# Splitting the solve's state in PSUM with TensorE and ScalarE, and reordering a unit's first steps, in a delta-rule attention and rational MoE kernel

## The chip, the cores and the metric

The kernel runs on one core of one Trainium2 chip. The metric is the device time of one execution in microseconds (us). Engines are named as the profile names them: PE is TensorE, DVE is VectorE, ACT is ScalarE, POOL is GpSimd, SP is the engine that issues most of the DMAs.

## The reference

Two layers follow each other. The first is a delta rule over 768 time steps, for 4 batches and 8 heads of width 48; its output, laid out as 3072 tokens of 384 numbers, goes through a two-layer network whose activation is a rational function.

```python
k_n = k / (np.linalg.norm(k, axis=-1, keepdims=True) + 1e-06)
for t in range(S):
    y[:, :, t] = np.einsum('bhd,bhde->bhe', q[:, :, t], state)
    v_old = np.einsum('bhde,bhd->bhe', state, kt)
    state = state + bt[:, :, :, None] * np.einsum('bhd,bhe->bhde', kt, vt - v_old)
...
h = x @ w_in
P = a[0] + a[1] * h + a[2] * h2 + a[3] * h3
Q = 1.0 + np.abs(b[0]) * np.abs(h) + np.abs(b[1]) * h2
g = P / (Q + 1e-06)
return (g @ w_out).astype(np.float32)
```

## The kernel before

**Numbers.** Almost every matmul is made of f16 operands that stand for f32 numbers: a value x is split into a first half hi = f16(x) and a second half lo = f16(x - hi), and a product is three matmul passes, hi*hi, lo*hi and hi*lo (`PASSES`). `split16` (line 223) writes the two halves: hi by ACT (line 228 or, with a scale, 230), lo by DVE or POOL (line 232 or, with a scale, 234). `mm3` (line 395) issues the three passes head by head, 48 matmuls for 16 (pair, head) slots; a pair is one half of the 4 batches, and each pair has its own PSUM bank.

**Chunks.** Time is cut into 12 chunks of 64 steps. In a chunk the delta rule becomes a triangular system, whose right side is the residual `rr` (from the values, less what the state gives for them). The diagonal 16x16 blocks of the system are inverted on DVE (`inverse`), and the solve goes through its four block rows. `solve_start` puts the product of `wbd` and `rr` into the PSUM tile `pu`. Then `solve_step` runs three times: it splits `pu`, scaled by the 0/1 column `zmask` that keeps one block row, into z (hi and lo), and adds the product of `ebd` and z to `pu` with 48 matmuls. `solved` splits the finished `pu` without a scale. `state_next` updates the state S from z (`pd`), and `outputs` makes y (`py`).

**From attention to tokens.** `tokens` finds the largest number in y (`xs`), makes from it the scale of the chunk, and transposes and splits y into `xT`. `scalars` then computes, in a row of some twenty operations on single columns that go back and forth between ACT (line 764) and DVE, the table `msc` (line 790) of per-column factors that every unit of this chunk needs.

**Units.** The network is cut into 96 units, 8 in each chunk, one for each 256 of the 2048 hidden columns. `hidden` is 18 matmuls into the PSUM tile `ph` (line 806). `numerator` makes from `ph` the start of numerator and denominator: u (lines 823, 826, 830) and w (825, 828, 829). `quotient` takes 1/Q as exp(-ln) on ACT (841, 842) and the two halves of g on DVE and POOL (845 to 853). `accumulate` is 12 matmuls into `po` (line 868).

**The order.** The code issues a unit's steps and pieces of the attention of later chunks in turns (`attention`, called once in each unit; `back` for the solve of the next chunk, with raised priority). The program's final order on each engine isn't the code's: a scheduler with a timeline of its own picks, engine by engine, the ready instruction of the highest priority, so a change in the kind or the order of a few instructions can move others. Each engine then works through its own list strictly in order. `ph` has two buffers, u, w and r have three each.

## Time and profile before

| | |
|---|---|
| median of 3 runs | 858.86 us (855.03 to 863.0) |
| the profiled execution | 857.44 us, with a span of 855.5 us |
| busy in the span | DVE 770.2, PE 624.5, ACT 593.4, POOL 467.6 us |
| mean granted clock of TensorE | 0.883 |

The span runs from the first to the last instruction; the profiled execution took 1.9 us more than it. From 0 to about 150 us the weights are loaded and split and chunk 0 is solved; the units run from about 150 us to the end. In a group's row stand the busy time in total, the mean of one instruction in ns, and after the bar the idle time of the engine just before these instructions with what ended it. Durations of neighbouring instructions overlap a little, so the mean of one times the count can exceed the busy time.

### The profile page before, as it was taken

The numbers are of one execution on the slowest core, as the hardware profiler recorded it, in microseconds if no ns is written. First come the engines' busy times: TensorE is split into PE (matmuls) and PEld (weight loads), VectorE is DVE, ScalarE is ACT, GpSimd is POOL, SyncE is SP. The second block draws the span as 40 slices with busy tenths as digits, with TensorE's granted clock in tenths as the row PEclk, the third lists the DMA queues.
The fourth block names the chain that finished last, engine by engine and source line by source line (L and its number), as shares of the span: only waits on it lengthen the run. The fifth ranks groups of instructions, "written<-read, shape, count | busy, mean of one in ns | idle before, by whom it ended". The sixth has DMA issues, their size and how long they took to land. (4 is left out here: it accounts for less than half of the span.)

```text
span 855.5 us, 23235 instructions
## 1 busy us (share of the span) xinstructions
PE 624.5 (73%) x9264; PEld 491.8 (57%) x9264; DVE 770.2 (90%) x1369; ACT 593.4 (69%) x1242; POOL 467.6 (55%) x430
## 2 busy tenths in 40 slices
PE   0230425865887697598878979888789889999885
PEld 0220424644666376476667757666677667776563
DVE  5999898899889969889899999998999998998896
ACT  4766666865666584685867777767768767887774
POOL 7665655454436345654764855746738455353622
PEclk9755555987899799889989999999989999999998
DMA  8997979966996976878879779579588572300000
GB/s 236 245 202 155 221 148 173 143 137 131 162 158 112 182 142 112 143 148 154 145 139 162 118 147 165 102 148 162 97 169 143 114 114 49 71 2 20 1 19 19
DMA packets 466508, 111.47 MB, mean 130 GB/s; under 512 B 431328, under 2 KB 463072, under 8 KB 466400
## 3 DMA queue, kind: packets, MB, share of 16 engines
q1 hardware_dynamic: 464224, 108.83, 68.5%
q8 instruction: 72, 1.18, 0.6%
q10 hardware_dynamic: 2176, 1.17, 0.4%
q14 instruction: 36, 0.29, 0.1%
HBM read 40.47 MB, written 26.23 MB: 78 GB/s over the span
## 5 line engine op out<-in xcount | busy, mean ns | idle before, releaser
L806 PE MATMUL ph<-xT,w_in 128*128 128x256 f16 x1728 | 225.6, 285 | 39.2 <-DVE mu L830 32.8
L868 PE MATMUL po<-w_out,mg 128*128 128x384 f16 x1152 | 219.0, 337 | 35.0 <-POOL mg L853 31.4
L806 PEld LDWEIGHTS <-w_in 128*128 128x128 f16 x1728 | 173.1, 102 | 76.7 <-DVE mu L830 34.9
L853 POOL TENSOR_TENSOR mg<-mu,mr 128x512 f16<-128x512 f32 x96 | 133.5, 1391 | 132.7 <-DVE mu L852 83.2
L868 PEld LDWEIGHTS <-mg 128*128 128x128 f16 x1152 | 109.3, 100 | 109.7 <-POOL mg L853 41.0
L823 ACT ACTIVATE mu<-ph,coef,msc 128x512 f32<-128x512 f32 x96 | 74.0, 771 | 49.4 <-POOL mg L853 20.2
L829 ACT ACTIVATE mw<-mw 128x512 f32<-128x512 f32 x96 | 60.4, 629 | 55.3 <-DVE mw L828 55.0
L848 DVE SCALAR_TENSOR_TENSOR mw<-mw,msc,mg 128x512 f32<-128x512 f32 x96 | 87.0, 907 | 0.7
L826 DVE TENSOR_TENSOR mu<-ph,mu 128x512 f32<-128x512 f32 x96 | 65.4, 681 | 19.4 <-ACT mr L825 14.0
L850 POOL TENSOR_TENSOR mu<-mu,mw 128x512 f32<-128x512 f32 x36 | 50.3, 1398 | 53.1 <-DVE mw L848 31.2
L403 PEld LDWEIGHTS <-kbd 128*128 128x128 f16 x1680 | 59.8, 102 | 25.5 <-issue 19.1
L828 DVE SCALAR_TENSOR_TENSOR mw<-mr,msc,ph 128x512 f32<-128x512 f32 x96 | 70.5, 735 | 0.0
L830 DVE SCALAR_TENSOR_TENSOR mu<-mu,msc,ph 128x512 f32<-128x512 f32 x96 | 70.4, 734 | 0.0
L841 ACT ACTIVATE mr<-mw,msc 128x512 f32<-128x512 f32 x96 | 69.0, 719 | 1.2
L403 PE MATMUL pu<-z,ebd 128*128 128x48 f16 x1728 | 53.7, 186 | 20.3 <-DVE z L234 14.9
L403 PEld LDWEIGHTS <-ebd 128*128 128x128 f16 x1728 | 52.8, 98 | 22.8 <-issue 21.5
L825 ACT ACTIVATE mr<-ph,msc 128x512 f32<-128x512 f32 x96 | 65.2, 679 | 0.0
L847 DVE SCALAR_TENSOR_TENSOR mg<-mu,msc,mr 128x512 f16<-128x512 f32 x60 | 59.3, 988 | 2.5 <-ACT mr L842 2.5
L842 ACT ACTIVATE mr<-mr 128x512 f32<-128x512 f32 x96 | 60.0, 625 | 1.1
L852 DVE SCALAR_TENSOR_TENSOR mu<-mu,msc,mw 128x512 f32<-128x512 f32 x60 | 55.7, 928 | 0.4
L403 PEld LDWEIGHTS <-wbd 128*128 128x128 f16 x1152 | 38.6, 101 | 28.3 <-issue 27.1
L232 POOL TENSOR_TENSOR mm<-m,mm 128x1024 f16<-128x1024 f32 x12 | 31.7, 2639 | 34.2 <-ACT mm L228 34.2
(198 smaller groups left out, 1313.7 us busy)
## 6 DMA issues: line engine op xcount, KB each, us to landing
wsi<-in_moe_w_in_dram SPq DMA_DIRECT2D x24, 256.0 KB, 5.2
xdk<-kn SPq DMA_DIRECT2D x24, 256.0 KB, 3.6
kbd<-tk SPq DMA_DIRECT2D x24, 256.0 KB, 4.5
gd<-g SPq DMA_DIRECT2D x24, 256.0 KB, 3.8
wso<-in_moe_w_out_dram SPq DMA_DIRECT2D x32, 192.0 KB, 3.8
xdq<-kn SPq DMA_DIRECT2D x24, 256.0 KB, 3.4
mbd<-mm SPq DMA_DIRECT2D x24, 256.0 KB, 5.8
wc<-img SPq DMA_DIRECT2D x24, 256.0 KB, 5.3
```

What stands on the lines that cost most here:

```text
L403: nc.tensor.matmul(dst[p][:, h], head(bd, lp, p * H + h), head(rt, rp, p * H + h), start=start and n == 0 and h == 0, stop=stop and n == l ...
L806: nc.tensor.matmul(ph[:, i], w_in[:, f2, wp, cc, i * P : (i + 1) * P], x[:, xp, cc], start=k == 0, stop=k == 3 * NCC - 1,)
L823: nc.scalar.activation(u, ph, AF.Identity, scale=A3, bias=a2)
L825: nc.scalar.activation(z, ph, AF.Abs, scale=B1)
L826: nc.vector.tensor_mul(u, ph, u)
L828: nc.vector.scalar_tensor_tensor(out=w, in0=z, scalar=B0, in1=ph, op0=ALU.add, op1=ALU.mult)
L829: nc.scalar.activation(w, w, AF.Abs)
L830: nc.vector.scalar_tensor_tensor(out=u, in0=u, scalar=A1, in1=ph, op0=ALU.add, op1=ALU.mult)
L841: nc.scalar.activation(r, w, AF.Ln, bias=Q0)
L848: nc.vector.scalar_tensor_tensor(out=w, in0=w, scalar=Q0, in1=g[:, 0], op0=ALU.add, op1=ALU.mult)
L853: nc.gpsimd.tensor_mul(g[:, 1], u, r)
L868: nc.tensor.matmul(po[p], g[:, gp, i, p * P : (p + 1) * P], w_out[:, f2, wp, i], start=f2 == lo and i == 0 and k == 0, stop=f2 == hi - 1 a ...
```

## The change

Three things are changed.

- The split of `pu` in the solve (three times in `solve_step`, once in `solved`). Before, ACT wrote hi and DVE computed lo from `pu` and hi. Now ACT writes hi, PE adds -hi to `pu` in place (one 128x384 matmul for each pair, with minus the identity as weights), ACT writes lo as a plain scaled copy of what is left in `pu`, the 48 matmuls of `mm3` follow, and in `solve_step` PE adds hi back to `pu` (two more matmuls, with the identity).
- The start of a unit. Before, ACT made u's first step and then |ph|, and DVE did u's product first. Now |ph| and w come first on both engines, and u follows.
- `mask` is BF16 instead of F32 and a new constant `minus16` is made once.

```diff
+    minus16 = cpool.tile([P, P], F16, name="minus16")
+    nc.vector.tensor_scalar(minus16, identf, -1.0, None, op0=ALU.mult)
...
-    mask = cpool.tile([P, C], F32, name="mask")
+    mask = cpool.tile([P, C], BF16, name="mask")
...
+    def plus(pu, sign, x):
+
+        for p in PAIRS:
+            nc.tensor.matmul(
+                pu[p].rearrange("x h d -> x (h d)"),
+                sign,
+                x[:, p * H : (p + 1) * H].rearrange("x h d -> x (h d)"),
+                start=False,
+                stop=True,
+                skip_group_check=True,
+            )
+
+    def split_in_psum(z, pu, by=1.0):
+
+        hi, lo = parts_by_pair(z)
+        nc.scalar.activation(hi, pu[2], AF.Copy, scale=by)
+        plus(pu, minus16, z[:, 0])
+        nc.scalar.activation(lo, pu[2], AF.Copy, scale=by)
...
-        split16(parts_by_pair(z), d["pu"][2], zmask[:, it : it + 1])
+        split_in_psum(z, d["pu"], zmask[:, it : it + 1])
         mm3(d["pu"], d["ebd"], z, start=False)
+        plus(d["pu"], ident16, z[:, 0])
...
-        split16(parts_by_pair(d["z"]), pu[2])
+        split_in_psum(d["z"], pu)
...
         ph = d.pop("ph")
+
+        r = z = sb.tile([P, 2, TG], F32, tag="mr", name=f"mr{n}", bufs=MB)
+        nc.scalar.activation(z, ph, AF.Abs, scale=B1)
+        w = sb.tile([P, 2, TG], F32, tag="mw", name=f"mw{n}", bufs=MB)
+        nc.vector.scalar_tensor_tensor(out=w, in0=z, scalar=B0, in1=ph, op0=ALU.add, op1=ALU.mult)
         u = sb.tile([P, 2, TG], F32, tag="mu", name=f"mu{n}", bufs=MB)
         nc.scalar.activation(u, ph, AF.Identity, scale=A3, bias=a2)
-        r = z = sb.tile([P, 2, TG], F32, tag="mr", name=f"mr{n}", bufs=MB)
-        nc.scalar.activation(z, ph, AF.Abs, scale=B1)
+        nc.scalar.activation(w, w, AF.Abs)
         nc.vector.tensor_mul(u, ph, u)
-        w = sb.tile([P, 2, TG], F32, tag="mw", name=f"mw{n}", bufs=MB)
-        nc.vector.scalar_tensor_tensor(out=w, in0=z, scalar=B0, in1=ph, op0=ALU.add, op1=ALU.mult)
-        nc.scalar.activation(w, w, AF.Abs)
         nc.vector.scalar_tensor_tensor(out=u, in0=u, scalar=A1, in1=ph, op0=ALU.add, op1=ALU.mult)
```

The scheduler's lists differ accordingly. In the rows below a name's last number is that of the buffer; `z_5_0` is the z of the first step in chunk 5, `mu37` is u of unit 37, `kp`, `sf` and `lgx` belong to the row of column operations before `msc`.

ACT at the first split of chunk 5, before (DVE's half of this split stands on DVE's list):

```order
L764 ACTIVATE kp_4_0_6409<-kp_4_0_6409,coef_99 128x1 x4
L230 ACTIVATE z_5_0_6591<-pu_5_6486,zmask_85 128x768
L842 ACTIVATE mr30_6471<-mr30_6471 128x512
L823 ACTIVATE mu31_6575<-ph_31_6556,coef_99,msc_3_5316 128x512
L825 ACTIVATE mr31_6577<-ph_31_6556,msc_3_5316 128x512
L764 ACTIVATE kp_4_0_6409<-kp_4_0_6409 128x1 x2
```

and now, where the two halves are lines 702 and 704:

```order
L702 ACTIVATE z_5_0_6663<-pu_5_6558,zmask_87 128x768
L786 ACTIVATE sf_4_6413<-sf_4_6413 128x2
L905 ACTIVATE ob_3_7171<-po_3_0_0_6247,kp_3_0_5352 128x384
L846 ACTIVATE mr32_6806<-ph_32_6787,msc_4_6503 128x512
L846 ACTIVATE mr33_6938<-ph_33_6919,msc_4_6503 128x512
L905 ACTIVATE ob_3_7171<-po_3_0_1_6248,kp_3_0_5352 128x384
L244 ACTIVATE sq1_7_6883,fs_7_6880<-v_7_6360 128x768
L704 ACTIVATE z_5_0_6663<-pu_5_6558,zmask_87 128x768
L521 ACTIVATE g_7_6768<-pg_7_6719 128x1024
L850 ACTIVATE mu32_6810<-ph_32_6787,coef_101,msc_4_6503 128x512
```

The split stood among the steps of unit 31, before the factors of chunk 4 were done; it now stands at unit 32, and six other instructions lie between its two halves.

DVE between the largest number of chunk 4 (`xs_4`) and its factors (`msc_4`), before: `xs_4` and the first 11 of the 42 rows between the two:

```order
L740 TENSOR_REDUCE xs_4_6340<-px_4_6343 1x1
L580 TENSOR_SCALAR wh_6_6168<-wt0_111 128x256
L852 SCALAR_TENSOR_TENSOR mu27_6208<-mu27_6208,msc_3_5316,mw27_6213 128x512
L845 TENSOR_TENSOR mg28_6404<-mu28_6322,mr28_6324 128x512
L826 TENSOR_TENSOR mu29_6392<-ph_29_6373,mu29_6392 128x512
L828 SCALAR_TENSOR_TENSOR mw29_6397<-mr29_6394,msc_3_5316,ph_29_6373 128x512
L581 SCALAR_TENSOR_TENSOR wh_6_6168<-wt0_111,wh_6_6168 128x256
L848 SCALAR_TENSOR_TENSOR mw28_6327<-mw28_6327,msc_3_5316,mg28_6404 128x512
L742 TENSOR_SCALAR xs_4_6340<-px_4_6343 128x1
L830 SCALAR_TENSOR_TENSOR mu29_6392<-mu29_6392,msc_3_5316,ph_29_6373 128x512
L826 TENSOR_TENSOR mu30_6469<-ph_30_6450,mu30_6469 128x512
L828 SCALAR_TENSOR_TENSOR mw30_6474<-mr30_6471,msc_3_5316,ph_30_6450 128x512
```

and now, the last 12 rows down to `msc_4`; ahead of them there are only `xs_4` and two more rows:

```order
L870 SCALAR_TENSOR_TENSOR mg31_6818<-mu31_6651,msc_3_5374,mr31_6647 128x512
L871 SCALAR_TENSOR_TENSOR mw31_6649<-mw31_6649,msc_3_5374,mg31_6818 128x512
L255 TENSOR_SCALAR sf_4_6413<-lgx4_6420 128x1
L783 RECIPROCAL kp_4_0_6481<-lgx4_6420 128x1
L875 SCALAR_TENSOR_TENSOR mu31_6651<-mu31_6651,msc_3_5374,mw31_6649 128x512
L766 RECIPROCAL sf_4_6413<-sf_4_6413 128x1
L236 SCALAR_TENSOR_TENSOR xT_4_6411<-px_4_6415,sf_4_6413,xT_4_6411 128x768
L794 RECIPROCAL kp_4_0_6481<-kp_4_0_6481 128x2
L801 TENSOR_SCALAR kp_4_0_6481<-kp_4_0_6481,top_140 128x1
L255 TENSOR_SCALAR kp_4_0_6481<-kp_4_0_6481 128x1
L805 RECIPROCAL kp_4_0_6481<-kp_4_0_6481 128x1
L812 TENSOR_TENSOR msc_4_6503<-tab_139,sf_4_6413 128x48
```

Before, the work of units 27 to 31 stood between them; now only the end of unit 31 does, and 13 rows in all.

ACT at one unit, 37, before:

```order
L823 ACTIVATE mu37_7507<-ph_37_7488,coef_99,msc_4_6431 128x512
L829 ACTIVATE mw36_7442<-mw36_7442 128x512
L825 ACTIVATE mr37_7509<-ph_37_7488,msc_4_6431 128x512
L841 ACTIVATE mr36_7439<-mw36_7442,msc_4_6431 128x512
L260 ACTIVATE lgx5_7463<-xs_5_7455 128x1
L842 ACTIVATE mr36_7439<-mr36_7439 128x512
L261 ACTIVATE lgx5_7463<-lgx5_7463,consts_95 128x1
L829 ACTIVATE mw37_7512<-mw37_7512 128x512
```

and now:

```order
L846 ACTIVATE mr37_7593<-ph_37_7574,msc_4_6503 128x512
L850 ACTIVATE mu37_7597<-ph_37_7574,coef_101,msc_4_6503 128x512
L851 ACTIVATE mw37_7595<-mw37_7595 128x512
L864 ACTIVATE mr37_7593<-mw37_7595,msc_4_6503 128x512
L865 ACTIVATE mr37_7593<-mr37_7593 128x512
```

|ph| (mr) now leads, and u's step stands between |ph| and the |w| that waits for DVE's w.

## The prediction

> **What bounds the kernel now.** I read the page first, then the windows, then the groups by line and shape, the waits, and single stretches of the timeline. The page gives each engine's busy time and, in 40 slices of 21.4 us, where it lies.
>
> ```profile
> PE 624.5 (73%) x9264; PEld 491.8 (57%) x9264; DVE 770.2 (90%) x1369; ACT 593.4 (69%) x1242; POOL 467.6 (55%) x430
> ...
> DVE  5999898899889969889899999998999998998896
> ...
> PEclk9755555987899799889989999999989999999998
> ```
>
> DVE is busy nine tenths of the span in almost every slice; no other engine comes near. The windows (columns: window, us, busy us and count of PE, PEld, DVE, ACT, POOL, granted clock, DMA share, GB/s) show the same for the long middle, for a dense stretch in it, and for the end:
>
> ```profile
> 180.00:740.00 560.00, 458.75 (x7288) 364.64 (x7285) 512.67 (x830) 396.21 (x789) 311.03 (x251) 0.92 0.76 136
> ...
> 420.00:500.00 80.00, 66.21 (x1091) 52.80 (x1089) 77.20 (x127) 60.36 (x127) 53.80 (x46) 0.96 0.76 133
> ...
> 800.00:856.00 56.00, 41.28 (x280) 26.99 (x280) 44.00 (x63) 33.93 (x63) 18.89 (x15) 0.94 0.06 15
> ```
>
> In the middle DVE works 512.7 of 560 us (92%), PE 458.8 (82%), ACT 396.2 (71%). So DVE sets the pace, with PE second and not far behind. How long a chunk takes can be read from the state update, once in a chunk:
>
> ```profile
> L708 DVE SCALAR_TENSOR_TENSOR S<-pd,sc,S x10: 1003/1006/1018, 197.6 to 730.4; 128x768 f32<-128x768 f32 x10
> ```
>
> Nine periods in 730.4 - 197.6 = 532.8 us make 59.2 us for one chunk. By the shares of the middle, DVE works 54.2 us of that, PE 48.5 and ACT 41.9.
>
> **The change, part by part.** The groups of the split, of the unit's first steps and of `mask`:
>
> ```profile
> L234 DVE SCALAR_TENSOR_TENSOR z<-pu,zmask,z 128x768 f16<-128x768 f32 x36 | 36.3, 1009 | 3.4 <-ACT z L230 3.2
> ...
> L232 DVE TENSOR_TENSOR z<-pu,z 128x768 f16<-128x768 f32 x12 | 11.4, 947 | 0.7 <-ACT z L228 0.7
> ...
> L230 ACT ACTIVATE z<-pu,zmask 128x768 f16<-128x768 f32 x36 | 32.0, 888 | 7.6 <-PE pu L403 7.6
> ...
> L228 ACT CAST z<-pu 128x768 f16<-128x768 f32 x12 | 9.6, 799 | 0.0
> ...
> L658 DVE TENSOR_TENSOR m<-pm,mask 128x1024 f32<-128x1024 f32 x12 | 14.6, 1213 | 0.0
> ...
> L826 DVE TENSOR_TENSOR mu<-ph,mu 128x512 f32<-128x512 f32 x96 | 65.4, 681 | 19.4 <-ACT mr L825 14.0 <-issue 1.9 <-POOL mg L853 1.6
> ...
> L823 ACT ACTIVATE mu<-ph,coef,msc 128x512 f32<-128x512 f32 x96 | 74.0, 771 | 49.4 <-POOL mg L853 20.2 <-PE ph L806 13.7 <-DVE msc L790 11.1
> ...
> L829 ACT ACTIVATE mw<-mw 128x512 f32<-128x512 f32 x96 | 60.4, 629 | 55.3 <-DVE mw L828 55.0
> ```
>
> *DVE's half of the split goes.* 36 instructions of 1009 ns and 12 of 947 ns leave DVE: 36.3 + 11.4 = **47.7 us**. DVE stood idle only 4.1 us ahead of them, so they lay on the pacing engine with nothing beside them. Per chunk that is 4.0 us, which leaves DVE 50.2.
>
> *ACT's second half comes.* The new instruction reads the same PSUM tile, with the same scale and type of output, as the first half. So it costs 36 x 888 + 12 x 799 = 41.6 us of ACT, which rises from 41.9 to 45.4 us a chunk. This lies beside DVE's work and still under it: **0** of its own. If that cover were gone, with ACT the pacing engine, it would be the whole 41.6. In the Trainium skill, "ScalarE: Activation LUTs", Rules for kernel authors, an add or a multiply belongs on VectorE and not on ScalarE, since VectorE is faster for each element. That speaks against this move, and the rows above don't bear it out for an f32 read from PSUM: 888 and 799 ns on ACT against 1009 and 947 on DVE. By that rule the term would be a loss in engine time; by the rows it is a small gain.
>
> *PE's matmuls come.* 48 splits with two matmuls each for -hi are 96, and 36 steps with two for +hi are 72: 168 of 128x384. Stretches of the timeline (start, length) give the price of the same size, and of a unit's first matmuls at full clock and behind a long idle:
>
> ```profile
> 400.89 2.11 PE L868 MATMUL po<-w_out,mg 128*128 128x384 f16 x12
> ...
> 408.08 2.13 PE L806 MATMUL ph<-xT,w_in 128*128 128x256 f16 x18
> ...
> 442.03 4.02 PE L806 MATMUL ph<-xT,w_in 128*128 128x256 f16 x18 [5.05 <-DVE mu L830]
> ```
>
> 2.11 / 12 = 176 ns each, 168 x 0.176 = 29.6 us in all, 2.5 a chunk. PE rises from 48.5 to 51.0 us a chunk and passes DVE's 50.2. So PE is what is late next, and its work isn't free. Its bounds are 0 (all in PE's idle time, 101 us of the middle) and 29.6 (all on the path). I take a third, **+10 us**, since PE was in work 82% of the middle but waited for others in the rest.
>
> *New waits in the split.* PE's -hi now waits for ACT's hi, and ACT's lo for PE's -hi; before there was one step, from hi to lo to the matmuls. The waits of the old split:
>
> ```profile
> PE pu L403 <- DVE z L234: 14.9, 8, 6.6
> ...
> ACT z L230 <- PE pu L403: 7.6, 4, 4.4
> ...
> PE pd L403 <- DVE z L232: 4.9, 3, 3.2
> ```
>
> With the 4.1 us on DVE these are 31.5 us in 48 splits, mostly on engines that could afford it. What is queued behind: on PE, in chunk 5's first step, the rest of `pg` and the 48 matmuls of the step; on ACT `g`, for which POOL waits, and u's first step, for which DVE waits. The scheduler put six other instructions between ACT's two halves there, about 4 us of cover by their groups, against 0.35 us for two matmuls. Bounds: 0 (the waits only change places), and 31.5 (they come a second time and all reach DVE). I take a fifth, **+6**.
>
> *The unit's first steps.* DVE's first step waited for two ACT instructions; now for one (|ph|), so each of DVE's 13 waits for ACT there (14.0 us) can be up to 0.77 us shorter, 10 us. ACT's 55.0 us ahead of |w| are covered by u's step (771 ns), but ACT doesn't pace. The bounds are -14 and 0, since no instruction is added; I take **-5**. In the last 56 us, where there is no solve, this is all that can act: DVE is idle 12 us there.
>
> *The factors of a chunk.* In the new list DVE has less to do between `xs` and `msc`: in chunks 1 to 5 there were 27, 18, 27, 43 and 51 rows from one to the other, and there are 19, 13, 15, 14 and 17. On the timeline the first of these stretches begins and ends with
>
> ```profile
> 213.70 0.27 DVE L740 TENSOR_REDUCE xs<-px 1x1 f32<-1x128 f32 x1
> ...
> 225.16 0.85 DVE L790 TENSOR_TENSOR msc<-tab,sf 128x48 f32<-128x48 f32 x1
> ```
>
> and the windows of all five are
>
> ```profile
> 213.70:225.20 11.50, 9.93 (x59) 6.36 (x60) 9.13 (x32) 7.28 (x26) 7.00 (x6) 0.66 0.89 159
> 290.50:306.00 15.50, 12.25 (x147) 9.36 (x148) 9.94 (x19) 9.97 (x30) 5.48 (x4) 0.69 1.02 176
> 350.20:372.70 22.50, 13.83 (x195) 11.37 (x196) 17.18 (x29) 15.50 (x38) 12.84 (x11) 0.77 0.77 142
> 406.70:436.10 29.40, 26.27 (x426) 21.21 (x425) 23.99 (x45) 23.06 (x55) 22.93 (x20) 1.00 0.79 135
> 463.30:495.70 32.40, 29.67 (x412) 22.96 (x410) 30.96 (x52) 25.77 (x59) 26.38 (x22) 1.00 0.79 131
> ```
>
> The chain took 11.5 us where it was shortest. DVE was idle in the five stretches for 2.4 + 5.6 + 5.3 + 5.4 + 1.4 = 20.1 us. For chunk 4's new list the groups give DVE's work:
>
> ```profile
> L830 DVE SCALAR_TENSOR_TENSOR mu<-mu,msc,ph 128x512 f32<-128x512 f32 x96 | 70.4, 734 | 0.0
> ...
> L847 DVE SCALAR_TENSOR_TENSOR mg<-mu,msc,mr 128x512 f16<-128x512 f32 x60 | 59.3, 988 | 2.5 <-ACT mr L842 2.5
> ...
> L848 DVE SCALAR_TENSOR_TENSOR mw<-mw,msc,mg 128x512 f32<-128x512 f32 x96 | 87.0, 907 | 0.7
> ...
> L852 DVE SCALAR_TENSOR_TENSOR mu<-mu,msc,mw 128x512 f32<-128x512 f32 x60 | 55.7, 928 | 0.4
> ...
> L234 DVE SCALAR_TENSOR_TENSOR xT<-px,sf,xT 128x768 f16<-128x768 f32 x12 | 12.1, 1011 | 4.0 <-ACT xT L230 4.0
> ...
> L783 DVE RECIPROCAL kp<-kp 128x1 f32<-128x1 f32 x13 | 2.0, 150 | 0.1
> ```
>
> 0.73 + 0.99 + 0.91 + 0.93 + 1.01 and eight column operations at about 0.15 make 5.8 us, so about 5.5 of 11.5 would be idle, 27.5 us in five chunks, 7 more than now. Bounds: 0 (the emptier chain runs faster) and 15 (double). I take **+7**.
>
> *The rest.* `mask` in BF16: DVE takes 1213 ns for 1024 elements, 1.18 a piece, and in L232's row, with an f16 operand beside f32 from PSUM, 947 / 768 = 1.23. A two-byte operand doesn't move the rate: 0. `minus16` is one 128x128 operation at the start, where L320 waits for POOL:
>
> ```profile
> L320 DVE TENSOR_SCALAR w_out<-wai 128x256 uint32<-128x256 uint32 x24 | 10.2, 428 | 4.7 <-POOL wai L319 4.7
> ```
>
> At most 0.4 us, hidden in that wait. No DMA and no POOL instruction is added. SP's list keeps its kinds but not its order; with a DMA share of 0.76 in the middle I put that at 0, for want of a row that prices it.
>
> The sum: -47.7 + 0 + 10 + 6 - 5 + 7 = **-29.7 us**. Against the profiled execution, 857.4 - 29.7 = 827.7. That execution lies 1.4 us under the median of the runs shown, so the time is **829 us**. As a check, 25 us over 11 chunks is a period near 57 us, with PE at 51.0 / 57 = 90% and DVE at 88%: less than DVE's 92% now, but with two engines close to each other.
>
> **The rivals.** *The attention's latency paces the first chunks.* In chunks 1 to 5 the new list shows a chain with little beside it, as above; then a DVE that has less to do just waits there longer, and only chunks 6 to 11 gain. 6 x 4.0 = 24 less half of the sum's other terms (18) is 15: 857.4 - 15, about 844 by the median. For it speaks that these stretches show DVE idle up to a third now (5.6 of 15.5); against it, that DVE is 97% busy from 420 to 500.
>
> *PE takes over the bound outright.* Full 29.6 us on the path, with the hops at half of their bound (15.8) and the chain's 7: -47.7 + 29.6 + 15.8 - 5 + 7 = 0, so 859, no change. For it: PE's 51.0 against DVE's 50.2. Against it: PE has idle time in every slice, and the windows show DVE at 97% with PE at 83% side by side, so such engines can overlap.
>
> *Slower: PE's -hi blocks its queue.* PE works in order. If ACT reaches hi late, everything behind -hi stands, `ph` and `po` too, and a stall ends with slow matmuls: in the row above 18 took 4.02 us after 5.05 us of idle, against 2.13, so 1.9 us more. The Trainium skill, "TensorE: Matmul & The Clock Gate", Part 1, has the array drop to half its clock after an idle window of about 3.4 us, and this row agrees. The rival needs more than (47.7 - 10 + 5 - 7) / 48 = 0.74 us of stall in each split that reaches the end; at 14.9 / 8 = 1.86 us for one of PE's old waits, that is 19 of the 48 splits. If six in ten wait so, 29 x 1.86 = 54 us give 857.4 - 35.7 + 54 = 875.7, or 877 by the median. Against it: of 48 old splits PE waited in 8.
>
> **How the numbers follow.** The forecast has 0.58, the latency rival 0.18, the PE bound 0.14, the blocked queue 0.10. The forecast's own range is 811 (PE's, the hops', the first steps' and the chain's terms all at 0) to 845 (PE's term at 20 and the hops' at 12). The range reaches over the latency rival and half of the PE bound, to 852; what it leaves out is the blocked queue, the other half of the PE bound and a small tail below. About 1% is what a measurement of this kernel can tell: 850.3 and 867.4. Below lie the forecast, 0.13 of the latency rival and 0.04 of the PE bound, 0.75. Within lie 0.05 of the latency rival, 0.09 of the PE bound and 0.01 of the last, 0.15. Above lies 0.10.
>
> **What would show it.** DVE's busy time should fall to 722 us, ACT's rise to about 635 and PE's by some 30. PE's share of the middle should be near DVE's. DVE's idle time ahead of u's and w's first steps should be no more than now, and between `xs` and `msc` of chunks 1 to 5 some 5 us each. The waits of `pu`'s matmuls for z should be near 20 us in total, not 50. I am wrong if DVE's idle time grows by as much as its work falls: in the chains to `msc`, then the second case holds; ahead of operations that wait for `ph`, the third; and where PE waits for hi, the fourth.

## The result, and the profile after

The changed kernel takes 890.45 us (median of 4 runs, 889.24 to 893.52) against 858.79 us before: 1.0372 times as long, with a 95% interval of 1.0335 to 1.0408. The prediction was 829 us. The profiled execution of the changed kernel took 889.75 us, with a span of 888.0 us. The page of the changed kernel, its busy times, DVE's slices and the chain that ended last:

```profile
PE 661.0 (74%) x9432; PEld 511.9 (58%) x9432; DVE 720.7 (81%) x1322; ACT 628.6 (71%) x1290; POOL 466.5 (53%) x430
...
DVE  5998997896888598599598497795697977778786
...
DVE 27%; PE 20%; ACT 16%; DMA 15%; SPq 9%; issue 8%; POOL 5%; POOLq 0%; ACTq 0%; DVEq 0%
```

DVE did lose its work: 770.2 - 720.7 = 49.5 us less. But the span grew by 32.5 us, so DVE's idle time grew by 82 us, from 855.5 - 770.2 = 85.3 to 888.0 - 720.7 = 167.3. Full slices have become sevens and eights, in every part of the span. The chain leads through all engines and through transfers; no engine has a third of it. The window of the long middle, which in before showed DVE with 512.67 us, and the state update, once in a chunk:

```profile
180.00:740.00 560.00, 457.66 (x6894) 357.53 (x6894) 449.80 (x759) 397.63 (x777) 298.88 (x241) 0.92 0.80 134
```

```profile
L730 DVE SCALAR_TENSOR_TENSOR S<-pd,sc,S x10: 992/1008/1017, 191.3 to 771.1; 128x768 f32<-128x768 f32 x10
```

In the middle nobody is above 82% now (PE 457.66 of 560, DVE 449.80, ACT 397.63), and fewer matmuls fit into it (6894 against 7288). Nine periods of the state update take 771.1 - 191.3 = 579.8 us instead of 532.8, so a chunk takes 64.4 us instead of 59.2. The whole result lies there: the first update comes 6.3 us earlier, the nine periods are 47.0 us longer, and what follows the last update is 8.2 us shorter (116.9 against 125.1), in sum 32.5 us.

The groups of the changed kernel that belong to the split and to a unit's first steps, and those of the factors' chain on DVE:

```profile
L704 ACT ACTIVATE z<-pu,zmask 128x768 f16<-128x768 f32 x36 | 32.4, 901 | 3.9 <-PE pu L690 3.8
L702 ACT ACTIVATE z<-pu,zmask 128x768 f16<-128x768 f32 x36 | 32.3, 898 | 4.3 <-PE pu L690 2.8 <-PE pu L405 1.5
L690 PE MATMUL pu<-z,minus 128*128 128x384 f16 x96 | 24.2, 332 | 25.0 <-ACT z L702 25.0
L690 PE MATMUL pu<-z,ident 128*128 128x384 f16 x72 | 19.2, 350 | 0.0
...
L848 DVE SCALAR_TENSOR_TENSOR mw<-mr,msc,ph 128x512 f32<-128x512 f32 x96 | 70.3, 740 | 20.2 <-ACT mr L846 18.9 <-PE pu L690 1.3
L852 DVE TENSOR_TENSOR mu<-ph,mu 128x512 f32<-128x512 f32 x96 | 65.5, 682 | 19.7 <-ACT mu L850 19.6
...
L255 DVE TENSOR_SCALAR sf<-lgx 128x1 uint32<-128x1 uint32 x12 | 1.8, 148 | 7.9 <-ACT lgx L263 7.8
L812 DVE TENSOR_TENSOR msc<-tab,sf 128x48 f32<-128x48 f32 x11 | 6.9, 629 | 7.3 <-ACT sf L786 7.3
L255 DVE TENSOR_SCALAR kp<-kp 128x1 uint32<-128x1 uint32 x13 | 1.9, 149 | 6.7 <-ACT kp L803 6.6
L801 DVE TENSOR_SCALAR kp<-kp,top 128x1 f32<-128x1 f32 x13 | 2.7, 211 | 6.5 <-ACT kp L786 6.5
```

DVE's waits ahead of a unit's first steps are 20.2 + 19.7 = 39.9 us, twice the 19.4 of before, and those in the factors' chain are 28.4 us. In before the same four groups of that chain had 3.7, 1.8 and 1.4 us and, for `sf`, less than 1:

```profile
L779 DVE TENSOR_SCALAR kp<-kp,top 128x1 f32<-128x1 f32 x13 | 2.7, 208 | 3.7 <-ACT kp L764 3.7
...
L253 DVE TENSOR_SCALAR kp<-kp 128x1 uint32<-128x1 uint32 x13 | 1.9, 144 | 1.8 <-ACT kp L781 1.8
...
L790 DVE TENSOR_TENSOR msc<-tab,sf 128x48 f32<-128x48 f32 x11 | 6.8, 621 | 1.4 <-ACT sf L764 1.4
```

The longest waits of the changed kernel that the change made:

```profile
ACT mu L850 <- DVE mw L848: 72.6, 53, 5.7
...
PE pu L690 <- ACT z L702: 25.0, 16, 3.0
...
PE pu L405 <- ACT z L704: 15.0, 12, 2.5
```

What a split has become is best seen on the timeline (start, length). The first split of chunk 5, changed kernel, from hi to the first of the 48 matmuls:

```profile
428.13 0.90 ACT L702 ACTIVATE z<-pu,zmask 128x768 f16<-128x768 f32 x1
...
429.02 0.81 PE L891 MATMUL po<-w_out,mg 128*128 128x384 f16 x4
...
429.67 0.64 PE L405 MATMUL pg<-tk,kbd 128*128 128x64 f16 x16
...
430.15 0.49 PE L690 MATMUL pu<-z,minus 128*128 128x384 f16 x2
430.19 1.26 ACT L846 ACTIVATE mr<-ph,msc 128x512 f32<-128x512 f32 x2
...
430.48 1.12 PE L405 MATMUL pg<-tk,kbd 128*128 128x64 f16 x32
...
431.33 0.59 ACT L905 ACTIVATE ob<-po,kp 128x384 f32<-128x384 f32 x1
...
431.79 0.86 ACT L244 ACTIVATE sq<-v 128x768 f32<-128x768 f32 x1
...
432.62 0.92 ACT L704 ACTIVATE z<-pu,zmask 128x768 f16<-128x768 f32 x1
...
433.58 0.59 PE L405 MATMUL pu<-z,ebd 128*128 128x48 f16 x17 [1.98 <-ACT z L704]
```

and the same split before:

```profile
420.07 0.88 ACT L230 ACTIVATE z<-pu,zmask 128x768 f16<-128x768 f32 x1
...
420.99 1.02 DVE L234 SCALAR_TENSOR_TENSOR z<-pu,zmask,z 128x768 f16<-128x768 f32 x1
...
422.34 1.37 PE L403 MATMUL pu<-z,ebd 128*128 128x48 f16 x48
```

From the start of hi to the matmuls it took 422.34 - 420.07 = 2.3 us before, 1.9 of it work; now it takes 433.58 - 428.13 = 5.5 us, of which the three steps work only 0.90 + 0.49 + 0.92 = 2.3. The rest is time in line: -hi stood behind `po` and `pg` on PE for 1.1 us after hi was done, and lo behind `mr`, `ob` and `sq` on ACT for 2.0 us after -hi was done. Over the splits of chunks 1 to 11 (43 of them can be told in the trace) the mean from hi to the matmuls is 4.8 us before and 6.3 us after. Four splits to a chunk make 19.0 and 25.1 us: 6.1 us more, where the period grew by 5.2.

### The profile page after: what moved, and what is told of

Read it like the earlier page. It is cut to its first block, busy times and chain, and to the rows that moved or that the text cites. A ratio compares the mean times of both kernels' runs of the same rounds, so it can differ in the third digit from the quotient of the medians.

```text
span 888.0 us, 23541 instructions
## 1 busy us (share of the span) xinstructions
PE 661.0 (74%) x9432; PEld 511.9 (58%) x9432; DVE 720.7 (81%) x1322; ACT 628.6 (71%) x1290; POOL 466.5 (53%) x430
## 4 chain that ended last, share of the span: by engine, by line
DVE 27%; PE 20%; ACT 16%; DMA 15%; SPq 9%; issue 8%; POOL 5%; POOLq 0%; ACTq 0%; DVEq 0%
PE ph L828 7%; PE po L891 5%; DVE mw L871 3%; DVE w_out L329 3%; DMA mbd<-mm 3%; DVE mg L870 3%; ACT mu L850 2%; DMA xdq<-kn 2%; DVE mw L848 2%; DVE mu L853 2%; DVE mu L875 2%; ACT mw L851 2%; DVE mu L852 2%; DMA tq<-xdq 2%; PE pu L405 1%
## 5 line engine op out<-in xcount | busy, mean ns | idle before, releaser
L828 PE MATMUL ph<-xT,w_in 128*128 128x256 f16 x1728 | 223.4, 283 | 24.8 <-DVE mu L853 20.0
L891 PEld LDWEIGHTS <-mg 128*128 128x128 f16 x1152 | 110.9, 100 | 98.0 <-POOL mg L876 24.4
L850 ACT ACTIVATE mu<-ph,coef,msc 128x512 f32<-128x512 f32 x96 | 74.9, 781 | 72.9 <-DVE mw L848 72.6
L405 PEld LDWEIGHTS <-kbd 128*128 128x128 f16 x1680 | 64.9, 107 | 38.9 <-issue 36.2
L848 DVE SCALAR_TENSOR_TENSOR mw<-mr,msc,ph 128x512 f32<-128x512 f32 x96 | 70.3, 740 | 20.2 <-ACT mr L846 18.9
L846 ACT ACTIVATE mr<-ph,msc 128x512 f32<-128x512 f32 x96 | 64.5, 683 | 30.6 <-PE ph L828 12.7
L852 DVE TENSOR_TENSOR mu<-ph,mu 128x512 f32<-128x512 f32 x96 | 65.5, 682 | 19.7 <-ACT mu L850 19.6
L870 DVE SCALAR_TENSOR_TENSOR mg<-mu,msc,mr 128x512 f16<-128x512 f32 x60 | 62.1, 1037 | 9.5 <-ACT mr L865 8.5
L857 POOL TENSOR_SCALAR mu<-mu,msc 128x512 f32<-128x512 f32 x36 | 30.1, 836 | 44.2 <-DVE mu L853 42.2
L405 PEld LDWEIGHTS <-wbd 128*128 128x128 f16 x1152 | 37.8, 101 | 26.2 <-issue 23.5
```

The costliest lines, as they stand in the source:

```text
L405: nc.tensor.matmul(dst[p][:, h], head(bd, lp, p * H + h), head(rt, rp, p * H + h), start=start and n == 0 and h == 0, stop=stop and n == l ...
L828: nc.tensor.matmul(ph[:, i], w_in[:, f2, wp, cc, i * P : (i + 1) * P], x[:, xp, cc], start=k == 0, stop=k == 3 * NCC - 1,)
L848: nc.vector.scalar_tensor_tensor(out=w, in0=z, scalar=B0, in1=ph, op0=ALU.add, op1=ALU.mult)
L850: nc.scalar.activation(u, ph, AF.Identity, scale=A3, bias=a2)
L852: nc.vector.tensor_mul(u, ph, u)
L870: nc.vector.scalar_tensor_tensor(out=g[:, 0], in0=u, scalar=A0, in1=r, op0=ALU.add, op1=ALU.mult)
```

## The experiments

Four explanations were open after the traces had been compared. First, that the unit's new order makes the engines wait for their turn at `ph`. Second, that PE's or ACT's additional work is the price. Third, that the scheduler's new lists are bad, with the split itself innocent. Fourth, that the split's longer way through two engines' queues makes the solve longer and that the solve paces the kernel. Later it was asked what ties one solve to the next. All ratios are against the kernel before, run on the same chip; the brackets are 95% intervals.

### The two parts apart

e1_split_only is the changed kernel with the unit's steps in the old order; e2_swap_only is the kernel before with only the new order:

```diff
+        r = z = sb.tile([P, 2, TG], F32, tag="mr", name=f"mr{n}", bufs=MB)
+        nc.scalar.activation(z, ph, AF.Abs, scale=B1)
+        w = sb.tile([P, 2, TG], F32, tag="mw", name=f"mw{n}", bufs=MB)
+        nc.vector.scalar_tensor_tensor(out=w, in0=z, scalar=B0, in1=ph, op0=ALU.add, op1=ALU.mult)
         u = sb.tile([P, 2, TG], F32, tag="mu", name=f"mu{n}", bufs=MB)
         nc.scalar.activation(u, ph, AF.Identity, scale=A3, bias=a2)
...
```

> The new split in PSUM with the unit's steps in their old order (u's first step, then |ph|, on ACT). Two theories for the loss of 32 us. Theory A, turns at ph: in the changed list ACT's u step waits for DVE's w (72.6 us in 53 waits in the profile of after), because ACT's two reads of ph now stand on both sides of a DVE read of it, and DVE's product then waits for ACT's u (19.6 us). By A this kernel is free of the loss and shows the gain of the split, about 830 to 845 us. Theory B, the solve's longer way: hi, -hi, lo, matmuls, +hi make the solve and with it the tokens of the next chunk later, and DVE waits between xs and msc. By B this kernel is as slow as the changed one, 880 to 895 us. In its list DVE has 14 to 21 rows between xs and msc, as few as the changed one.

> The old split (lo on DVE) with the unit's steps in their new order (|ph| and w lead, u follows). By theory A (turns at ph) this is slower than before by most of what the changed kernel lost and more, since DVE's work is not reduced: 880 to 900 us, with ACT's u waiting for DVE's w some 70 us in total. By theory B (the solve's longer way) it is within 1% of before, 850 to 867 us.

The split alone took 897.90 us, 1.0481 [1.0451, 1.0512]; the new order alone 849.17 us, 0.9907 [0.9877, 0.9938], which is faster than both kernels. Together the two parts add up to the change: 857.6 + 40.3 - 8.5 = 889.4 against 890.45. So the loss belongs to the split. The page and DVE's first steps in e2_swap_only:

```profile
PE 624.5 (74%) x9264; PEld 491.7 (58%) x9264; DVE 761.1 (90%) x1369; ACT 590.4 (70%) x1242; POOL 470.1 (56%) x430
...
DVE 43%; ACT 13%; PE 12%; DMA 11%; issue 8%; SPq 7%; POOL 4%; POOLq 0%; ACTq 0%; DVEq 0%
```

```profile
L826 DVE SCALAR_TENSOR_TENSOR mw<-mr,msc,ph 128x512 f32<-128x512 f32 x96 | 70.4, 738 | 9.0 <-ACT mr L824 8.9
...
L830 DVE TENSOR_TENSOR mu<-ph,mu 128x512 f32<-128x512 f32 x96 | 65.3, 681 | 5.1 <-ACT mu L828 4.2 <-POOL mm L232 0.7
```

There DVE's waits ahead of the first steps fall from 19.4 to 14.1 us, and DVE has much the largest part of the chain. The doubling to 39.9 in the changed kernel comes with the split: e1_split_only has 38.0 us there.

But the shorter waits aren't what e2 gained. Its span is 846.4 us, so DVE is idle for 846.4 - 761.1 = 85.3 us in all, as in before; the 9.1 us are busy time, 770.2 against 761.1, with the same 1369 instructions. Single groups moved both ways. The one that fell most is a product in the units, shown in before and in e2:

```profile
L845 DVE TENSOR_TENSOR mg<-mu,mr 128x512 f16<-128x512 f32 x36 | 37.8, 1050 | 8.2 <-ACT mr L842 8.0 <-POOL mu L834 0.2
```

```profile
L846 DVE TENSOR_TENSOR mg<-mu,mr 128x512 f16<-128x512 f32 x36 | 30.2, 838 | 5.1 <-ACT mr L843 4.3 <-POOL mu L835 0.7
```

Why it takes less time in the new order was not tried.

### The turn at `ph`

e3_split_reads_first is e1 with ACT's two reads of `ph` (|ph| and u) ahead of DVE's w; e4_reads_first_only is the same order in the kernel before. ACT's u can't come to wait for DVE's w in this order. The edit of e4:

```diff
+        r = z = sb.tile([P, 2, TG], F32, tag="mr", name=f"mr{n}", bufs=MB)
+        nc.scalar.activation(z, ph, AF.Abs, scale=B1)
         u = sb.tile([P, 2, TG], F32, tag="mu", name=f"mu{n}", bufs=MB)
         nc.scalar.activation(u, ph, AF.Identity, scale=A3, bias=a2)
-        r = z = sb.tile([P, 2, TG], F32, tag="mr", name=f"mr{n}", bufs=MB)
-        nc.scalar.activation(z, ph, AF.Abs, scale=B1)
-        nc.vector.tensor_mul(u, ph, u)
         w = sb.tile([P, 2, TG], F32, tag="mw", name=f"mw{n}", bufs=MB)
...
         nc.scalar.activation(w, w, AF.Abs)
+        nc.vector.tensor_mul(u, ph, u)
```

> The new split, and a unit in which the denominator leads but both of ACT's reads of ph (|ph|, then u's step) come before DVE's first read. By theory A the wait of ACT's u for DVE's w is gone and with it the loss: 825 to 845 us. By theory B as slow as the changed kernel, 880 to 895 us.

> The old split, and the unit with both of ACT's reads of ph first, |ph| ahead of u's step, and DVE's w ahead of its product. By theory A no turn is taken at ph and DVE waits for one ACT step less than before at its w: 850 to 862 us. By theory B the units' order does not matter: 853 to 865 us. It serves as the pair of the run with the new split: their difference is the split alone, in this order of steps.

887.91 us, 1.0369 [1.031, 1.0428], and 856.56 us, 0.9989 [0.9966, 1.0011]. Without the 72.6 us of that wait the new split is as slow as with it, and with the old split the order with the wait is the faster one. The first explanation falls.

### The residual's second half

`rr` is split by ACT and POOL. e5_split_rr_dve (from e1) and e6_before_rr_dve (from before) let DVE take POOL's half:

```diff
-        split16(parts(d["rr"]), rf, eng=nc.gpsimd)
+        split16(parts(d["rr"]), rf)
```

> The new split with the old unit order (897.9 us before this edit), and the second half of the residual rr, a step of the same loop from one state S to the next, is computed by DVE instead of POOL. It adds 12 DVE operations (about 11 us) and takes a slower one off the loop. Theory B (the loop through the solve sets the pace, DVE has time to spare): faster, 870 to 890 us, though DVE does more. Theory C (the load of the engines sets the pace, PE's 168 matmuls or ACT's 41 us): no gain, 895 to 910 us.

> The kernel before with the same edit on rr alone. Theory B with DVE as the pace of the kernel before: DVE's 11 us more are paid, 858 to 870 us, not faster. If the loop paces the kernel before too: faster, 840 to 852 us.

899.15 us, 1.0473 [1.044, 1.0506], and 868.00 us, 1.011 [1.0083, 1.0137]. In e5 the stretch that this was to shorten, from the residual to the first hi, went from 11.8 to 12.4 us in the mean of chunks 2 to 11 (in e5 a single one of 29.6 us pulls it up), so the run says little about the solve's length. Nor are e6's 9 us more the added work on DVE: its busy time is 768.8 us against 770.2, and its idle time 96.6 against 85.3.

### The load

e7_lo_on_dve is e1 with lo read by DVE, so that DVE has its work back and ACT has none added; -hi stays on PE. e8_pe_only is the kernel before with PE's matmuls of -hi and hi around the steps' `mm3` (144 of the 168), where they cancel and lo doesn't wait for -hi; the constant and `mask` are those of the change.

```diff
-        nc.scalar.activation(lo, pu[2], AF.Copy, scale=by)
+        nc.vector.tensor_scalar(lo, pu[2], by, 0.0, op0=ALU.mult, op1=ALU.add)
```

```diff
         split16(parts_by_pair(z), d["pu"][2], zmask[:, it : it + 1])
+        plus(d["pu"], minus16, z[:, 0])
         mm3(d["pu"], d["ebd"], z, start=False)
+        plus(d["pu"], ident16, z[:, 0])
```

> The new split with the old unit order, but the second half is read from PSUM by DVE and not by ACT: the way through PE is as long, ACT's 41 us are gone and DVE's 48 operations are back. Theory B (the way's length): as slow or slower, 890 to 915 us. Theory C, if ACT's load is the cause: back near before, 853 to 868 us.

> The old split (lo on DVE from pu and hi), and PE's -hi and +hi added in the solve's steps behind lo, around the 48 matmuls: 144 of the 168 new matmuls with no engine waiting for PE between the halves. Theory C, if PE's load is the cause: 880 to 900 us. Theory B: only some 0.7 us a step lies on the loop, 858 to 875 us.

The pages of e7_lo_on_dve and e8_pe_only, and the matmuls' groups in e8_pe_only:

```profile
PE 660.8 (74%) x9432; PEld 510.6 (57%) x9432; DVE 758.0 (85%) x1370; ACT 597.2 (67%) x1242; POOL 472.1 (53%) x430
```

```profile
PE 646.7 (75%) x9408; PEld 504.3 (59%) x9408; DVE 763.0 (89%) x1370; ACT 593.5 (69%) x1242; POOL 471.7 (55%) x430
```

```profile
L690 PE MATMUL pu<-z,minus 128*128 128x384 f16 x72 | 19.3, 352 | 18.2 <-DVE z L236 9.6 <-DVE sw L255 8.5
L690 PE MATMUL pu<-z,ident 128*128 128x384 f16 x72 | 18.9, 346 | 0.0
```

e7 took 888.62 us, 1.0346 [1.0308, 1.0385]. Against e1, which has DVE at 728.6 and ACT at 633.6 us, it has 36 us less on ACT and 29.4 us more on DVE, and the two together bring 9 of e1's 40 us back; what each does alone can't be told from one run. e8 took 862.26 us, 1.0048 [1.002, 1.0077], with 38.2 us of such matmuls: some 4 us. So PE's load isn't the price. The clearest pair is e7 and e8: neither has ACT's additional work, and by their pages the engines are busy for nearly the same time, within 5 us on DVE, ACT and POOL and 14 us on PE; yet e7 takes 26 us more. So ACT's load isn't most of the price either, and the second explanation falls. What e1, e7 and the changed kernel share, and e8 has not, is that lo waits for -hi and -hi for hi. The lists of the two differ as well.

### The dose

e9_swap_last_only is the changed kernel with the split in PSUM only in `solved` (12 of 48 splits), e10_swap_steps_only only in the steps (36 of 48). e12_pairs splits pair by pair, with 96 ACT instructions more, so that a split passes through more places in the queues.

```diff
-        split_in_psum(z, d["pu"], zmask[:, it : it + 1])
+        split16(parts_by_pair(z), d["pu"][2], zmask[:, it : it + 1])
         mm3(d["pu"], d["ebd"], z, start=False)
-        plus(d["pu"], ident16, z[:, 0])
```

```diff
-        split_in_psum(d["z"], pu)
+        split16(parts_by_pair(d["z"]), pu[2])
```

```diff
-        nc.scalar.activation(hi, pu[2], AF.Copy, scale=by)
-        plus(pu, minus16, z[:, 0])
-        nc.scalar.activation(lo, pu[2], AF.Copy, scale=by)
+        for p in PAIRS:
+            nc.scalar.activation(hi[:, p], pu[p], AF.Copy, scale=by)
+            plus(pu, minus16, z[:, 0], (p,))
+        for p in PAIRS:
+            nc.scalar.activation(lo[:, p], pu[p], AF.Copy, scale=by)
```

> A dose of the new split: in the changed kernel only the last split of a chunk's solve (12 of 48) is done in PSUM, the three steps are the old way. With 0 of 48 the time was 849.2 us, with 48 of 48 890.5. Theory B (a loop through the solve that has some slack while DVE paces; the first hops fit in it, and DVE is relieved of 11 us): 838 to 852 us. A price for each split alike (0.86 us each): 859 us.

> The other part of the dose: the three steps of a chunk's solve in PSUM (36 of 48), the last split the old way. Theory B with slack: the slack is used up, 862 to 885 us. A price for each split alike: 880 us.

> The changed kernel with each split taken pair by pair: hi of pair 0, hi of pair 1, -hi of each behind its hi, then lo of each, 384 columns at a time, so that PE's -hi of one pair lies beside ACT's hi of the other. 96 more ACT instructions (some 17 us of ACT). In its list DVE has almost no unit rows between xs and msc. If what counts is the shortest way through a split on the chip: faster than the changed kernel, 865 to 885 us. If what counts is how often a split has to queue behind other work: as slow or slower, 888 to 910 us.

873.55 us, 1.0154 [1.0101, 1.0207]; 873.49 us, 1.0178 [1.0131, 1.0225]; 940.71 us, 1.0946 [1.0899, 1.0992]. The state update in e12_pairs:

```profile
L732 DVE SCALAR_TENSOR_TENSOR S<-pd,sc,S x10: 1002/1010/1018, 210.3 to 827.2; 128x768 f32<-128x768 f32 x10
```

Its period is 68.5 us. The table sets the kernels side by side. The third column is four times the mean from hi's start to the next matmuls, the fourth is a ninth of the way from the first to the last update of S.

| kernel | us | hi to matmuls, us a chunk | period of S, us |
|---|---|---|---|
| e2_swap_only | 849.2 | 15.8 | 58.6 |
| e4_reads_first_only | 856.6 | 18.1 | 59.9 |
| before | 858.8 | 19.0 | 59.2 |
| e8_pe_only | 862.3 | 19.7 | 58.7 |
| e6_before_rr_dve | 868.0 | 20.6 | 58.7 |
| e9_swap_last_only | 873.6 | 20.6 | 62.2 |
| e10_swap_steps_only | 873.5 | 23.0 | 62.9 |
| e5_split_rr_dve | 899.2 | 24.8 | 64.5 |
| changed kernel | 890.5 | 25.1 | 64.4 |
| e3_split_reads_first | 887.9 | 25.2 | 63.9 |
| e1_split_only | 897.9 | 25.3 | 65.0 |
| e7_lo_on_dve | 888.6 | 25.9 | 62.8 |
| e11_priority (below) | 885.7 | 26.6 | 64.2 |
| e18_after_py_late (below) | 885.4 | 27.8 | 63.1 |
| e12_pairs | 940.7 | 37.8 | 68.5 |

The three kernels with `py` moved from the start and the two without the carrying of S, all below, are left out, since they differ in more than this. From no split in PSUM to 12 or 36, to all 48, and to the way made longer still, both the time and the stretch from hi to the matmuls rise. But the price isn't one for each split: against e2, 12 splits cost 24.4 us and the other 36 cost 24.3, where all 48 cost 41.3. From e2 to the changed kernel 9.3 us a chunk, over ten chunks 93 us, cost 41.3; from there to e12 12.7 us a chunk cost 50. So some four tenths of what the stretch grows arrive at the end. The stretch isn't a dial that was turned by itself, either: in e9, where the three steps of a chunk are as in e2, they too take longer, 4.8 us each against 3.7. Among the kernels with all 48 splits in PSUM, which lie within 3 us of each other in the third column, the time doesn't follow it; and e12 has 17 us more work on ACT as well. The table shows the size of the effect; it isn't a law, and it doesn't prove by itself that the stretch is the cause.

### The order of the lists

e11_priority is e1 with ten times the raise in priority for the solve, at all six places where it is given:

```diff
-            with tc.high_priority(300):
+            with tc.high_priority(3000):
```

> The new split with the old unit order (897.9 us), and the solve's priority in the scheduler raised from 300 to 3000: the operations and their hops are the same, only their places in the lists move, and in six middle chunks the list again has 11 to 24 unit rows between xs and msc on DVE instead of 7 to 11. If the lists' order alone makes the loss: most of it goes, 860 to 875 us. If the way's length on the chip makes it: 885 to 900 us.

885.65 us, 1.031 [1.0277, 1.0343], 12 us less than e1. The lists matter, but the greater part of e1's 40 us stays; the stretch from hi to the matmuls didn't get shorter (26.6 against 25.3 us), so what was won was won elsewhere. So the third explanation accounts for less than a third of e1's loss, as far as this one reordering can show; other lists were not tried.

### What ties one solve to the next

A longer solve need not cost anything if two solves can overlap. Two ties were tried. One is S: e13_after_cut (from the changed kernel) and e14_before_cut (from before) write the update over `pd` instead of S, so they leave out the carrying of the state beyond chunk 0.

```diff
-                out=by_pair(S16), in0=pd[2], scalar=d["isv"], in1=by_pair(S16), op0=ALU.mult, op1=ALU.add
+                out=pd[2], in0=pd[2], scalar=d["isv"], in1=by_pair(S16), op0=ALU.mult, op1=ALU.add
```

> The changed kernel with the loop over chunks cut: the update of the state S is computed as before, but written back to PSUM and not carried on, so from chunk 2 on every chunk is solved with the S of chunk 0 (left out: the carrying on of S, and with it what y owes to it). All instructions are there. If the loop S - residual - solve - S paces the changed kernel: 820 to 850 us, under the cut kernel of before by the DVE work that went. If the splits' waits hold up the queues whatever the loop does: 875 to 895 us, and above the cut kernel of before by as much as without the cut.

> The kernel before with the same cut (S is not carried on). DVE paces it: 845 to 860 us, little changed. If the loop had a part in its pace already: 820 to 845 us.

897.51 us, 1.0469 [1.0449, 1.0489], and 849.75 us, 0.9913 [0.9893, 0.9932]. The changed kernel isn't paced by the loop over S alone. The other tie is the one PSUM tile of the pool `ps_c`, which `pk`, `pu`, `pd` and `py` of each chunk use in turn; by the starts and ends of what touches it, `pu` holds it 32.5 us a chunk before and 38.9 after. e15_after_py, e16_before_py and e17_swap_py (from the changed kernel, from before, from e2) take `py` out of this round; e18_after_py_late does so from chunk 3 on.

```diff
-        py = bank(ps_c, f"py_{c}", D)
+        py = bank(ps_f, f"py_{c}", D)
```

```diff
-        py = bank(ps_c, f"py_{c}", D)
+        py = bank(ps_c if c < 3 else ps_f, f"py_{c}", D)
```

> The changed kernel with py, the PSUM tile of a chunk's outputs, in the buffer of the pool ps_f instead of ps_c's. Theory P (the single buffer of ps_c, used in turn by pk, pu, pd and py, paces the changed kernel): it takes about 7 us a chunk off the turn, 845 to 875 us. If the splits' waits hold up the engines' queues: 880 to 900 us.

> The kernel before with the same edit. Theory P: the buffer is free 23% of the middle and DVE paces, so little is gained, 850 to 865 us. If it is faster by as much as the changed kernel is with this edit, theory P does not tell the two apart.

> The old split, the new unit order (849.2 us) and py in ps_f. Theory P: as in the kernel before, little is gained: 840 to 855 us. It is a candidate for a version that beats both kernels.

> The changed kernel, but py of chunks 3 to 11 in the tile that px uses, so that from chunk 3 on the solve's tile is held by pk, pu and pd alone; nothing at the start is moved. If the time that the solve's one PSUM tile is held sets the period: py's hold of 5.4 us and one of the gaps leave the round, the 27.6 us that the same edit in all chunks won from unit 8 to unit 88 come back for 8 of 10 chunks, and there is no loss at the start: 862 to 875 us, with a period of S near 61 us instead of 64.4. If the hold only goes along with the period, and something else (a chain of waits through DVE and ACT, or the engines' load) sets it: 885 to 900.

The first three take longer than the kernels that they are made from: 923.46 us, 1.0778 [1.0736, 1.082]; 902.28 us, 1.0523 [1.0494, 1.0552]; 897.73 us, 1.0468 [1.0442, 1.0493]. e16 and e15 lose 48 and 60 us once, at the start, where chunk 1's `py`, by the order of the lists, has to wait for its turn in the other pool: unit 8's product of `ph` and u on DVE comes at 281.0 us instead of 233.1 in e16, and at 283.2 instead of 223.3 in e15. From unit 8 to unit 88 the changed kernel needs 623.2 us and e15 595.6, while before and e16 need 579.0 and 578.1. I read this as 27.6 us won by the freer tile, and e18 was to show it without the loss at the start. It didn't: 885.37 us, 1.0311 [1.0268, 1.0354], 5 us less than the changed kernel, with intervals that still overlap. The state update and two waits of e18_after_py_late:

```profile
L730 DVE SCALAR_TENSOR_TENSOR S<-pd,sc,S x10: 1006/1014/1021, 192.1 to 760.1; 128x768 f32<-128x768 f32 x10
```

```profile
PE pu L405 <- ACT z L704: 10.7, 10, 2.6
...
PE pu L690 <- ACT z L702: 9.2, 7, 2.4
```

The period fell from 64.4 to (760.1 - 192.1) / 9 = 63.1 us, with 11.8 us won in nine periods, of which 7.3 were given back behind the last update (124.2 us instead of 116.9). So taking py's turn of 5.4 us a chunk out of the tile gains little; meanwhile the stretch from hi to the matmuls grew from 25.1 to 27.8 us, so it is no clean test of the tile. The 27.6 us of e15 were mostly the start: there unit 8 came 59.9 us later, the third update of S only 43.7 us later (314.1 against 270.4), so the solve was further ahead of the units when the count began; its period, 63.9 us, had hardly changed.

What stays open is why the solves can't overlap enough to hide the longer split. Breaking the loop over S alone, or taking `py` alone out of the tile, doesn't free them. Both at once was not tried, nor were the other things that neighbouring chunks share: the two buffers of z, which `rr` uses too, and the transfers of the attention's operands, with 15% of the chain for DMA and 9% for SP's queue.

## Why the prediction was wrong, step by step

**What bounds the kernel now: half right.** With the old split, e2 and e14 have 9.1 and 9.8 us less work on DVE than before, and spans 9.1 and 9.0 us shorter. Even there DVE's work isn't all: e6 and e8 have no more of it than before, and spans 9.9 and 3.0 us longer. But the step from there to "DVE's 47.7 us come off the time" failed. The changed kernel has 49.5 us less of it and 82 us more idle time, and e7, with 29.4 us more on DVE than e1, takes no longer. The Trainium skill, "Perfetto Trace Analysis", Identifying the Most-Contended Engine, says to look for the engine with the highest occupancy and to optimize that first. In e2 and e14 less work on that engine and less time go together, which agrees; in the change they don't: 49.5 us less on the engine with 90% came with a kernel 3.7% slower.

**New waits in the split: the step that failed.** The prediction took +6 us, and 31.5 at most, from the idle time that the old split's waits showed. Idle time isn't what a split costs. Each change of engine puts the next step into a queue that works strictly in order, and while it stands there that engine is busy with other work: in the split shown above, 3.1 of 5.5 us. The list of waits shows this only where the engine behind runs dry, as PE did there for 1.98 us. The prediction even counted the six instructions between ACT's halves as cover for the matmuls; they were 2.0 us of delay for lo. The change replaced ACT, DVE, PE by ACT, PE, ACT, PE, and the measured price, from e2 to the changed kernel, is 41.3 us where the prediction had -47.7 + 10 + 6 + 7 = -24.7. How the 66 us between the two divide into DVE's gain that didn't come and the longer solve's own cost isn't shown. That the split costs it is shown by e1 and e2; that it does so by its longer way rests on e7 against e8 and on the other explanations being too small.

**DVE's work, ACT's work.** The sizes were right: DVE was to have 722 us and has 720.7, ACT about 635 and has 628.6, at 898 to 901 ns a read against the 888 of the row used. That ACT's work costs nothing isn't quite borne out: with most of it gone again, and DVE's back, e7 is 9 us faster than e1.

**PE's matmuls.** The price of one was right. The groups have 24.2 + 19.2 = 43.4 us for the 168, which is 258 ns each, but matmuls overlap and a pair's row ends with the run-out of its second: in the stretch above the pair has 0.49 us, and PE's next matmuls start 0.33 us after it began, 165 ns for each. PE's busy time as a whole grew by 661.0 - 624.5 = 36.5 us. e8 prices 144 of the matmuls at some 4 us of time, so the term of +10 was too large: PE had room.

**The unit's first steps.** -5 was the right sign and near the size: e2 gained 8.5 us, and the changed kernel is 7.4 us faster than e1. DVE's waits there did fall in e2, to 14.1 us from 19.4, but its idle time as a whole did not fall, and the gain is shorter work on DVE, which the prediction didn't have. So the size was in part luck. That the waits were to be no more than now failed in the changed kernel (39.9), because of the split.

**The factors' chain.** It was put at +7 with 15 as its bound. In the five stretches that it was worked out from, from `xs` to `msc` of chunks 1 to 5, it was right: DVE is idle there for 29 us now, where the prediction had 27.5, against 20 before. But chunks 6 to 11 were left out of the account, and there the idle time in these stretches rose from 14 to 43 us. The four groups of the chain quoted above show 28.4 us of DVE idle time against fewer than 8, some 20 more. As DVE's work no longer sets the pace, I read this as the place where its spare time shows, not as a price of its own; no run tested it.

**The rivals.** "PE's -hi blocks its queue" had the right sign, and its signal came: 40 us of waits for z, where the forecast had "near 20, not 50". (Of the old splits PE waited in 11 by the prediction's own rows, 8 for a step's z and 3 for the last one's, where it counted 8.) But its price, stall by stall, isn't the cause. In e18 the same waits are 19.9 us and the time 885.37. PE as the bound is refuted by e8 and by PE's 82% of the middle, the same as before. The latency rival named the right kind of thing, a chain with little beside it, but in the wrong place (the factors of five chunks) and with a gain left over. The prediction's signs for telling the rivals apart didn't do so: DVE's idle time grew both in the chains to `msc` and ahead of the steps that read `ph`, and PE's waits for hi grew too.

## What to carry to other kernels

Before work is moved off the busiest engine, follow the chain that the moved step belongs to, and count its changes of engine: each costs a place in an in-order queue, time in which that engine is busy and which a list of waits shows only in part. Read it on the timeline, from the first step's start to the consumer's start, and price a longer chain by that stretch, not by the idle time at its ends. And make the two halves of a combined change apart: here one half was a gain of 0.9% that the other hid.

## What the runs showed that had not been expected

ACT's u waits for DVE's w in the new order (72.6 us in 53 waits), though it doesn't use w. Both read the same PSUM tile `ph`, and the program lets one engine at a time at it. The Trainium skill, "PSUM — Partial Sum Buffer", PSUM bank collisions raise a hardware error, says that two engines must not touch one bank at the same time, not even when both only read; the wait in the trace agrees with that, and no run here shows what happens without it. In these kernels the wait cost nothing that can be measured, as e2 and e3 show.

Busy time divided by the count overstates a short group of matmuls. Those of -hi and +hi have 252 and 267 ns each by their groups, while 12 in a row of the same size have 176 in the row that the prediction used; yet in the stretch shown PE went on 165 ns a matmul after the pair of -hi began, since the next group starts before the last matmul of the pair has ended.
